# Attention with two gated layers on one core: a part of the probability transposes moved from the DMA queue to TensorE and ScalarE, with a new order

## The chip, the cores and the metric

The kernel runs on one core of a Trainium2 chip. The metric is the device time of one execution in microseconds. Engines: TensorE (PE in the profile), VectorE (DVE), ScalarE (ACT), GpSimd (POOL), and SyncE (SP), which here issues all DMA transfers.

## What is computed

```python
q_pool = q.reshape(B, H, S // 2, 2, D).mean(axis=3)          # B, H, S, D = 4, 8, 1152, 64
scores = D ** -0.5 * np.matmul(q_pool, k.transpose(0, 1, 3, 2))
scores = scores - np.max(scores, axis=-1, keepdims=True)
attn = np.exp(scores)
attn = attn / (np.sum(attn, axis=-1, keepdims=True) + 1e-09)
x = np.matmul(attn, v)                        # then (B, S/2, H, D) as 2304 tokens of 512
h = x @ w_in                                  # 512 -> 2048
x = (h * np.cos(h)) @ w_out                   # 2048 -> 512
return ((x @ w_a) * (x @ w_b)) @ w_out2       # 512 -> 1536 -> 512
```

## The kernel before

The run has two parts. In the **attention part** two heads form a pair p (16 pairs), and a pair has nine tiles of 128 pooled queries by 1152 keys; tile t (0 to 143) is number k = t % 9 of its pair, and the fifth (k = 4) has rows of both heads. Numbers are kept in two pieces, a high one and the rest (`kh`/`kl`, `vh`/`vl`), and products are summed over the pieces.

A tile goes through these steps, whose names are also those of the tasks:

- `s` (L316, TensorE): scores into one of two PSUM buffers of three banks, six products of 384 columns (twelve for k = 4).
- `max` (L324, VectorE), `exp` (L331, ScalarE, with the row sum; for half of the tiles it stays in the PSUM buffer, `in_psum`, t % 4 < 2, for the others it goes to SBUF as `pf`), `r1`/`r2` (VectorE, the reciprocal of the sum).
- `ph` (L346, ScalarE): the high half of the probabilities in f16, and `pl` (L350, VectorE): the low half. Both lie in one buffer `phl`, [128, 2, 1152]; there are four such buffers, so `ph` of a tile waits for the transpose of the tile four before.
- `tr` (L357, issued by SP): one DMA transpose of the whole `phl`, 18 blocks of 128x128, into `pt`, where the keys lie on the partitions. It also waits for the `av` of the pair before, which reads the same columns of `pt`.
- `av` (L373, TensorE): probabilities times values, twice per pair, 54 products each, from `pt` and `vh`/`vl`; read out by `avhi` (L383, ScalarE) and `avlo` (L392, VectorE) into the tokens `xt`.

Scores of tile t need the PSUM buffer of tile t - 2 back, from `pl` where the exponential stays in PSUM and from `exp` otherwise. Beside this run the loads of q, k, v (`qst`, `kst`, `vst`) with their splitting on GpSimd, VectorE and ScalarE (`kdup`, L222, is ScalarE's copy of k), the loads and conversion of `w_in` (`w`), and, from the fifth pair on, the first layer `h` (L448 to L450, TensorE, 12 products a group, 92 of its 128 groups here), read out by `ho` (L490) and stored by `hput` (L497). The groups of `av`, `h` and a small one for v share two PSUM slots (`mm_tile`): a third group waits until the first has been read out.

The **dense part** does the rest of the layers on TensorE; its code is not touched.

What sets the order: each step is a task with an engine, a cost and a due time, t plus a number of the table `DUE`. `Dag.run` plays the tasks through with these costs; whenever an engine is free it takes, of the tasks that are ready, the one that is due first, and the instructions are written in that order. On the chip each engine, and SP's queue, then goes through its list strictly in order; what is ready but stands behind a waiting instruction waits too. Groups in the two slots are tasks with `mm`.

Of the kernel before, what the change touches and what calls it, by code (L numbers as in the profile page):

```python
# [10 lines left out]
F16 = mybir.dt.float16  # L11
I32 = mybir.dt.int32
I64 = mybir.dt.int64
AF = mybir.ActivationFunctionType
ALU = mybir.AluOpType
# [10 lines left out]


DUE = dict(
    prep0=-6.24, prep1=-6.1, ldq=-38.55, ldk=-36.98, kd=-30.41, ldv=-79.38, qs=-131.27, vabs=17.17, vhi=75.51,
    vlo=70.05, max=-17.99, r=-31.13, exp=-1.94, ph=-23.98, pl=-7.26, tr=-30.08, av=-8.92, avh=22.89, avp=-196.82,  # L30
    xhi=-16.15, xlo=119.2, h=22.48, hrel=-90.16, whi=-65.72, wlo=-25.78, ho=-72.2, hput=60.89, w=51.54, slack=74.26,
    wstep=91.4
)


# [79 lines left out]
def kernel(  # L115
# [12 lines left out]
    nc = tc.nc  # L128
# [8 lines left out]
    TILES = 9  # L137
# [43 lines left out]
    def mm_tile(name):  # L181
        p = mm_slots[mm_at[0] % len(mm_slots)]
        mm_at[0] += 1
        return p.tile([128, 512], F32, tag="mm", name=name)
# [15 lines left out]

    ident = k_p.tile([128, 128], F32, name="ident")
    ones = k_p.tile([128, 128], F32R, name="ones")

    def v_const():
        nc.gpsimd.memset(ident, 1.0)
        nc.gpsimd.tensor_scalar(ones, ident, 1.0, 1.0, op0=ALU.mult, op1=ALU.mult)
        nc.gpsimd.affine_select(
            out=ident, in_=ident, pattern=[[-1, 128]], compare_op=ALU.is_equal,
            fill=0.0, base=0, channel_multiplier=1,
        )  # L210

    def load_k(p):
        b, pr = divmod(p, NP)
# [135 lines left out]
    def emit_pl(t):  # L349
# [2 lines left out]
            op0=ALU.mult, op1=ALU.subtract,  # L352
        )

    def emit_tr(t):
        k = t % TILES
        nc.sync.dma_start_transpose(  # L357
            out=pt[:, :, 128 * k:128 * k + 128],
            in_=phl_t.pop(t).rearrange("p a b c -> p (a b c)"),
        )  # L360

    av_ps = {}

# [143 lines left out]
    for c in range(C1):  # L507
        stages = convert(
            w_in[c], lambda: wf_p.tile([128, 512], F32, tag="wf", name="wf"),
            lambda t, c=c: w1.update({("i", c): t}), False,  # L510
        )
        at = DUE["w"] + DUE["wstep"] * c
        add(("w", c, 0), "SP", 1750, at, stages[0], deps=[("w", c - 1, 4)], wait=DMA_WAIT)
        for i, (eng, cost) in enumerate((("ACT", 650), ("DVE", 410), ("DVE", 680), ("DVE", 680))):
            deps = [("w", c, i)] + ([("w", c - 2, 3)] if i == 0 else [])
            add(("w", c, i + 1), eng, cost, at + 1 + i / 4, stages[i + 1], deps=deps, port=i > 0)
# [4 lines left out]
    for p in range(NPAIR):  # L521
        t0 = TILES * p
        b, pr = divmod(p, NP)
        for key, fn, cost, at, prev, free in (
            (("q", p), load_q, 2700, DUE["ldq"], ("v", p - 1), [("qlo", p - 1, 1)]),
            (("k", p), load_k, 2400, DUE["ldk"], ("q", p), [("klo", p - 1, 1), ("kdup", p - 1, 1)]),
            (("v", p), load_v, 2400, DUE["ldv"], ("k", p), [("vlo", p - 1)]),
        ):
            add(key, "SP", cost, t0 + at, fn, p, deps=free, after=[prev], wait=DMA_WAIT)
        add(("qs", p), "POOL", 1550, t0 + DUE["qs"], q_sum, p, deps=[("q", p)], slack=DUE["slack"])  # L530
# [16 lines left out]
        for k in range(TILES):  # L547
            t = t0 + k
            deps = [("pl" if in_psum(t - 2) else "exp", t - 2)]
            for j in ((0, 1) if k == 4 else (k // 5,)):  # L550
                deps += [("klo", p, j), ("kdup", p, j), ("qlo", p, j)]
            add(("s", t), "PE", (2100 if k == 4 else 1060) * (1.25 if p >= NP else 1.6), t, emit_s, t, deps=deps, after=[("s", t - 1)])
            add(("max", t), "DVE", 1340, t + DUE["max"], emit_max, t, deps=[("s", t)])
            stored = [u for u in range(t) if not in_psum(u)]
            free = [] if in_psum(t) or len(stored) < NPB else [("pl", stored[-NPB])]
            add(("exp", t), "ACT", 1420, t + DUE["exp"], emit_exp, t, deps=[("max", t)] + free)
            add(("r1", t), "DVE", 140, t + DUE["r"], emit_r1, t, deps=[("exp", t)])
            add(("r2", t), "DVE", 150, t + DUE["r"], emit_r2, t, deps=[("r1", t)])
            add(("ph", t), "ACT", 1240, t + DUE["ph"], emit_ph, t, deps=[("r2", t), ("tr", t - NPHL)], after=[("ph", t - 1)])
            add(("pl", t), "DVE", 1390, t + DUE["pl"], emit_pl, t, deps=[("ph", t)], port=not in_psum(t))  # L560
            deps = [("pl", t)]
            deps.append(("av", p - 1, 0 if k in (0, 1, 5) else 1))
            add(("tr", t), "SP", 3050, t + DUE["tr"], emit_tr, t, deps=deps, wait=DMA_WAIT)
        for hf in range(2):
            at = t0 + TILES + DUE["av"] + DUE["avh"] * hf
            deps = [("tr", t0 + k) for k in ((0, 1, 2, 4, 5, 6), (2, 3, 4, 6, 7, 8))[hf]]
            deps += [("vhi", p), ("vlo", p)]
            if b > 1:
                deps.append(("h", C1 * (b - 1) - 1, 1))
# [17 lines left out]
    for m in range(2 * H_CUT):  # L587
# [9 lines left out]
        deps = [("h", n, hf)] + ([("hput", n - NST)] if hf == 0 else [("ho", n, 0)])  # L597
        add(("ho", n, hf), "ACT", 400, at + DUE["ho"], h_out, n, hf, deps=deps, slack=DUE["slack"] / 4)
        if hf == 1:
            add(("hput", n), "SP", 1100, at + DUE["hput"], h_put, n, deps=[("ho", n, 1)], wait=DMA_WAIT)  # L600
    for n in range(H_CUT, H_CUT + 2):
        w_need(n)
    dag.run()
# [338 lines left out]
```

## Time and profile before

| | us |
|---|---|
| median of 3 runs | 1412.39 (1410.11 to 1415.44) |
| the profiled execution | 1420.35 |
| its span, first to last instruction | 1418.6 |

The profile is of one execution. Busy times are of engines that work side by side, so they don't add up to the span. A wait is put down to what ended it last; the chain of waits follows back from the last instruction what released each step. The DMA share is a mean over the 16 DMA engines of the time that their packets took; packets overlap, so it can pass 1. For SP's queue a transpose's time is how long it held the queue, and the landing is counted from its issue. The granted clock is a share of 2.4 GHz, at which TensorE runs at most; 0.5 is 1.2 GHz, the only other level seen here.

### The profile page before, as it was taken

To read this page: it belongs to the slowest core of one execution; us is meant where nothing else is said; L and a number is where in the kernel's file an instruction comes from. 1 tells how busy PE (TensorE), PEld (TensorE's weight loads), DVE (VectorE), ACT (ScalarE), POOL (GpSimd) and SP (SyncE) were. 2 spreads that over 40 slices of the span, in tenths; PEclk is the share of its full clock that TensorE was granted. 3 is DMA by queue.
4 is the path that set the end of the run, shared out by engine and by line. 5 is a ranking of instruction groups with operands and counts; after the bars stand their busy time and mean duration, and the time that the engine had idled before them with its cause. 6 is when DMAs were issued, how large, how long until landed. Compare 5 with 4: busy or idle time off the path is not lost.

```text
span 1418.6 us, 20183 instructions
## 1 busy us (share of the span) xinstructions
PE 1217.2 (86%) x7768; PEld 1139.6 (80%) x7768; DVE 905.2 (64%) x1304; ACT 755.9 (53%) x1134; POOL 415.1 (29%) x319
## 2 busy tenths in 40 slices
PE   3456668967689778976999999999999999999998
PEld 2445558856589768966999999999999999999997
DVE  6788888787878868887589999987411212111111
ACT  4567767776778657776486767764311111111111
POOL 5242334634437445640203434333100000000000
PEclk9668789988889989998999999999999999999999
DMA  5899999999989989998875466544010101010000
GB/s 169 162 190 206 199 197 203 229 222 192 217 174 232 220 172 213 212 229 157 247 233 164 155 196 201 192 152 135 30 67 0 67 1 67 0 67 0 23 1 23
DMA packets 380930, 206.33 MB, mean 145 GB/s; under 512 B 340641, under 2 KB 352929, under 8 KB 380321
## 3 DMA queue, kind: packets, MB, share of 16 engines
q1 hardware_dynamic: 380832, 205.03, 60.3%
q8 instruction: 61, 1.00, 0.3%
q14 instruction: 37, 0.29, 0.1%
HBM read 90.18 MB, written 29.88 MB: 85 GB/s over the span
## 4 chain that ended last, share of the span: by engine, by line
PE 61%; DVE 13%; issue 4%; ACT 3%; DMA 1%; POOL 1%; SPq 0%; DVEq 0%; ACTq 0%; POOLq 0%
PE s L316 6%; PE av L373 4%; DVE phl L350 4%; PE pa L448 4%; PE pa L450 4%; PE pa L449 4%; PE pb L450 4%; PE pb L449 4%; PE pb L448 4%; PE o L450 4%; PE o L449 4%; PE o L448 3%; PE h L448 3%; PE h L450 3%; PE h L449 3%
## 5 line engine op out<-in xcount | busy, mean ns | idle before, releaser
L316 PE MATMUL s<-kh,tq 128*128 128x384 f32 x480 | 190.7, 397 | 144.5 <-DVE phl L350 92.1
L316 PEld LDWEIGHTS s<-kh,tq 128*128 128x128 f32 x480 | 105.1, 219 | 167.4 <-issue 107.2
L718 DVE TENSOR_TENSOR pv<-pb,av 128x384 f32<-128x384 f32 x72 | 40.2, 558 | 300.5 <-PE pb L450 298.1
L324 DVE TENSOR_REDUCE nm<-s 128x1 f32<-128x1152 f32 x144 | 193.0, 1352 | 45.1 <-PE s L316 44.8
L316 PE MATMUL s<-kl,tq 128*128 128x384 f32 x480 | 181.1, 377 | 0.0
L448 PE MATMUL h<-xt,whl 128*128 128x288 f32 x512 | 156.6, 306 | 11.0 <-DVE vma L280 5.1
L450 PE MATMUL h<-xt,whl 128*128 128x288 f32 x512 | 154.7, 302 | 2.4 <-POOL whl L467 2.3
L449 PE MATMUL h<-xt,whl 128*128 128x288 f32 x512 | 154.2, 301 | 0.0
L714 ACT ACTIVATE av<-pa 128x384 f32<-128x384 f32 x72 | 35.5, 493 | 204.9 <-PE pa L450 204.8
L448 PE MATMUL x<-gh,w 128*128 128x384 f32 x384 | 130.6, 340 | 5.6 <-DVE x2t L686 5.6
L449 PE MATMUL x<-gl,w 128*128 128x384 f32 x384 | 130.5, 340 | 3.2 <-DVE gl L655 3.2
L331 ACT ACTIVATE pf<-s,nm 128x1152 f32<-128x1152 f32 x72 | 88.0, 1223 | 81.6 <-DVE nm L324 81.2
L450 PE MATMUL x<-gh,w 128*128 128x384 f32 x384 | 130.1, 339 | 0.0
L350 DVE SCALAR_TENSOR_TENSOR phl<-pf,rc,phl 128x1152 f16<-128x1152 f32 x72 | 119.8, 1671 | 9.4 <-ACT phl L346 9.3
L373 PE MATMUL av<-pt,vh 128*64 128x288 f16 x1152 | 121.2, 301 | 4.0 <-DMA pt<-phl 3.8
L722 ACT ACTIVATE ph<-pv 128x384 fp32r<-128x384 f32 x72 | 37.9, 527 | 145.9 <-DVE pv L718 145.9
L350 DVE SCALAR_TENSOR_TENSOR phl<-s,rc,phl 128x1152 f16<-128x1152 f32 x72 | 100.9, 1412 | 22.7 <-ACT phl L346 22.5
L448 PEld LDWEIGHTS h<-xt,whl 128*128 128x128 f32 x512 | 99.7, 195 | 14.0 <-issue 9.9
L316 PEld LDWEIGHTS s<-kl,tq 128*128 128x128 f32 x480 | 106.1, 221 | 0.0
L450 PEld LDWEIGHTS h<-xt,whl 128*128 128x128 f32 x512 | 99.4, 194 | 3.5 <-POOL whl L467 3.4
L331 ACT ACTIVATE s<-s,nm 128x1152 f32<-128x1152 f32 x72 | 85.8, 1192 | 28.3 <-DVE nm L324 27.0
L449 PEld LDWEIGHTS h<-xt,whl 128*128 128x128 f32 x512 | 99.7, 195 | 0.0
(88 smaller groups left out, 3208.1 us busy)
## 6 DMA issues: line engine op xcount, KB each, us to landing
h_d<-hs SPq DMA_DIRECT2D x64, 288.0 KB, 2.7
gf<-h_d SPq DMA_DIRECT2D x48, 384.0 KB, 3.4
raw<-in_w_out_dram SPq DMA_DIRECT2D x28, 512.0 KB, 4.1
qst<-in_qT_dram SPq DMA_DIRECT2D x16, 640.0 KB, 4.9
kst<-in_kT_dram SPq DMA_DIRECT2D x16, 576.0 KB, 5.0
vst<-in_vP_dram SPq DMA_DIRECT2D x16, 576.0 KB, 4.7
raw<-in_w_in_dram SPq DMA_DIRECT2D x16, 512.0 KB, 4.1
raw<-in_w_a_dram SPq DMA_DIRECT2D x12, 512.0 KB, 4.3
```

The costliest lines, as they stand in the source:

```text
L316: nc.tensor.matmul(ps[:, c, :N3], lhs, kx[:, c * N3:(c + 1) * N3], start=(i == 0), stop=(i == len(terms) - 1),)
L324: nc.vector.tensor_reduce(nm, s_t[t][:, :, :N3], op=ALU.max, axis=AX.XY, negate=True)
L331: nc.scalar.activation(pf, ps, AF.Exp, bias=m_t.pop(t), scale=1.0, accum_out=rs)
L350: nc.vector.scalar_tensor_tensor(phl_t[t][:, 1], e_t.pop(t)[0], rc_t.pop(t), phl_t[t][:, 0], op0=ALU.mult, op1=ALU.subtract,)
L373: nc.tensor.matmul(ps[64 * j:64 * j + 64, :NH], vx[:, kt, 64 * j:64 * j + 64], pt[:, o + kt, c0:c0 + NH], start=(kt == 0 and i == 0), stop ...
L448: nc.tensor.matmul(ps, lh, rh, start=first, stop=False)
L449: nc.tensor.matmul(ps, lh, rl, start=False, stop=False)
L450: nc.tensor.matmul(ps, ll, rh, start=False, stop=last)
L714: nc.scalar.activation(ab_t["a"], p_ps.pop("a")[:, :T2], AF.Copy, scale=W_INV)
L718: nc.vector.tensor_tensor(ab_t[at, c], p_ps.pop("b")[:, :T2], ab_t.pop("a"), op=ALU.mult)
L722: nc.scalar.activation(ph_t[at, c][:, 0], ab_t[at, c], AF.Copy)
```

## The change

In every third tile (t % 3 == 2, 48 of 144) the DMA transposes only the low half, nine blocks. The high half is transposed by TensorE: three groups `tp` of three products each, the 128x128 block as the stationary operand times a f16 identity (`ident16`, made once on GpSimd), into one of the two shared PSUM slots; ScalarE copies each group, 128x384, into `pt` (`te`). A group needs only `ph`, not `pl`. `ph` of a tile that reuses the buffer waits for the products as well as for the transpose, and `av` waits for the copies. The code also allows the low half (with VectorE), which is not used.

The planner's costs of SP's transfers are raised (a whole transpose 3050 to 3350, a half 1700; loads of q, k and v by 300, of w by 350, stores by 250), and nearly all numbers of `DUE` are different, so that every engine's order changes. The lines that matter:

```diff
 DUE = dict(
-    prep0=-6.24, prep1=-6.1, ldq=-38.55, ldk=-36.98, kd=-30.41, ldv=-79.38, qs=-131.27, vabs=17.17, vhi=75.51,
+    prep0=-9.26, prep1=2.27, ldq=-30.55, ldk=-36.98, kd=-30.63, ldv=-67.47, qs=-117.71, vabs=22.98, vhi=69.7,
...
+    wstep=44.21, tp=0.33, te=-16.64,
 )
...
+    ident16 = k_p.tile([128, 128], F16, name="ident16")
...
+        nc.gpsimd.tensor_scalar(ident16, ident, 1.0, 1.0, op0=ALU.mult, op1=ALU.mult)
...
+    def by_pe(t):
+        return (0,) if t % 3 == 2 else ()
+
     def emit_tr(t):
         k = t % TILES
-        nc.sync.dma_start_transpose(
-            out=pt[:, :, 128 * k:128 * k + 128],
-            in_=phl_t.pop(t).rearrange("p a b c -> p (a b c)"),
-        )
+        cols = slice(128 * k, 128 * k + 128)
+        if by_pe(t):
+            nc.sync.dma_start_transpose(
+                out=pt[:, KT:, cols], in_=phl_t[t][:, 1].rearrange("p b c -> p (b c)")
+            )
+        else:
+            nc.sync.dma_start_transpose(
+                out=pt[:, :, cols], in_=phl_t[t].rearrange("p a b c -> p (a b c)")
+            )
+
+    def emit_tp(t, e, i):
+        tp_ps[t, e, i] = mm_tile("tp")
+        for n in range(3):
+            cols = slice(128 * n, 128 * n + 128)
+            nc.tensor.matmul(
+                tp_ps[t, e, i][:, cols], phl_t[t][:, e, i, cols], ident16, start=True, stop=True
+            )
+
+    def emit_te(t, e, i):
+        k = t % TILES
+        src = tp_ps.pop((t, e, i))[:, :384].rearrange("p (n c) -> p n c", n=3)
+        dst = pt[:, e * KT + 3 * i:e * KT + 3 * i + 3, 128 * k:128 * k + 128]
+        if e == 0:
+            nc.scalar.activation(dst, src, AF.Copy)
+        else:
+            nc.vector.tensor_scalar(dst, src, 1.0, None, op0=ALU.mult)
...
-        add(("w", c, 0), "SP", 1750, at, stages[0], deps=[("w", c - 1, 4)], wait=DMA_WAIT)
+        add(("w", c, 0), "SP", 2100, at, stages[0], deps=[("w", c - 1, 4)], wait=DMA_WAIT)
...
-            (("q", p), load_q, 2700, DUE["ldq"], ("v", p - 1), [("qlo", p - 1, 1)]),
+            (("q", p), load_q, 3000, DUE["ldq"], ("v", p - 1), [("qlo", p - 1, 1)]),
...
-            add(("tr", t), "SP", 3050, t + DUE["tr"], emit_tr, t, deps=deps, wait=DMA_WAIT)
+            if len(by_pe(t)) < 2:
+                add(("tr", t), "SP", 1700 if by_pe(t) else 3350, t + DUE["tr"], emit_tr, t, deps=deps, wait=DMA_WAIT)
+            for e in by_pe(t):
+                for i in range(3):
+                    add(("tp", t, e, i), "PE", 300, t + DUE["tp"] + i / 10, emit_tp, t, e, i,
+                        deps=[("pl" if e else "ph", t), ("tp", t, e, i - 1), deps[1]], mm=("te", t, e, i))
+                    add(("te", t, e, i), "DVE" if e else "ACT", 450, t + DUE["te"] + i / 10, emit_te, t, e, i,
+                        deps=[("tp", t, e, i), deps[1]])
...
+            deps += [("te",) + d[1:] + (e, i) for d in deps for e in range(2) for i in range(3)]
...
-            add(("hput", n), "SP", 1100, at + DUE["hput"], h_put, n, deps=[("ho", n, 1)], wait=DMA_WAIT)
+            add(("hput", n), "SP", 1350, at + DUE["hput"], h_put, n, deps=[("ho", n, 1)], wait=DMA_WAIT)
```

The two other loads, k and v, change as the load of q does, and `ph` gets the products of the tile four before among its dependencies.

Two places show how the order moves. First SP's queue from the transpose of tile 94 to the load of k for pair 12 (`kst`); `x2` counts equal rows, `128x18x128` is a whole transpose, `128x9x128` a half. Before (the rows ahead of these are stores of `h`):

```order
L357 DMA_TRANSPOSE pt<-phl 128x18x128 x2
L255 DMA vst<-in_vP_dram 128x1152
L357 DMA_TRANSPOSE pt<-phl 128x18x128 x2
L231 DMA qst<-in_qT_dram 128x1280
L357 DMA_TRANSPOSE pt<-phl 128x18x128 x3
L215 DMA kst<-in_kT_dram 128x1152
L497 DMA h_d_60<-hs 128x576
```

Now (from the transposes of tiles 93 and 94 on):

```order
L370 DMA_TRANSPOSE pt<-phl 128x18x128 x2
L526 DMA h_d_60<-hs 128x576 x2
L366 DMA_TRANSPOSE pt<-phl 128x9x128
L370 DMA_TRANSPOSE pt<-phl 128x18x128
L257 DMA vst<-in_vP_dram 128x1152
L370 DMA_TRANSPOSE pt<-phl 128x18x128
L526 DMA h_d_60<-hs 128x576
L366 DMA_TRANSPOSE pt<-phl 128x9x128
L233 DMA qst<-in_qT_dram 128x1280
L370 DMA_TRANSPOSE pt<-phl 128x18x128 x2
L217 DMA kst<-in_kT_dram 128x1152
```

The load of k stays behind the transpose of tile 100, but two of the seven transposes from tile 94 on are halves; the load of v moves behind tile 96, and three stores of `h` stand among them.

Second ScalarE, from the exponential of tile 100 on; `phl` is a high half, `hs` a read-out of `h`, `xt` one of `av`. Before:

```order
L331 ACTIVATE s,rs<-s,nm 128x3x384
L346 ACTIVATE phl<-pf,rc 128x1152
L331 ACTIVATE s,rs<-s,nm 128x3x384
L383 ACTIVATE xt_2_119<-av,viv 128x288
L346 ACTIVATE phl<-s,rc 128x1152 x2
L331 ACTIVATE pf,rs<-s,nm 128x1152 x2
L346 ACTIVATE phl<-pf,rc 128x1152
```

Now (`pt<-tp` is the copy of a transposed group):

```order
L333 ACTIVATE s,rs<-s,nm 128x3x384
L412 ACTIVATE xt_2_119<-av,viv 128x288
L387 ACTIVATE pt<-tp 128x3x128
L348 ACTIVATE phl<-pf,rc 128x1152
L348 ACTIVATE phl<-s,rc 128x1152
L387 ACTIVATE pt<-tp 128x3x128 x2
L333 ACTIVATE s,rs<-s,nm 128x3x384
L519 ACTIVATE hs<-h 128x288
L348 ACTIVATE phl<-s,rc 128x1152
L412 ACTIVATE xt_2_119<-av,viv 128x288
L387 ACTIVATE pt<-tp 128x3x128
```

The copies of tile 98 stand between the exponentials of tiles 100 and 101, one ahead of two high halves and two directly ahead of the exponential.

## Rows read from the trace of the kernel before

**Rows 1.** The page, parts 1 and 2: busy time by engine; granted clock and DMA by slice.
```profile
PE 1217.2 (86%) x7768; PEld 1139.6 (80%) x7768; DVE 905.2 (64%) x1304; ACT 755.9 (53%) x1134; POOL 415.1 (29%) x319
...
PEclk9668789988889989998999999999999999999999
DMA  5899999999989989998875466544010101010000
```

**Rows 2.** Stretches of the run, columns named in the header row.
```profile
core 0: us, PE busy (x) PEld busy (x) DVE busy (x) ACT busy (x) POOL busy (x), PEclk, DMA share, GB/s
27.00:212.00 185.00, 109.35 (x732) 94.17 (x733) 154.80 (x230) 123.20 (x159) 58.64 (x39) 0.76 0.94 191
212.00:400.00 188.00, 143.73 (x1055) 130.52 (x1054) 155.89 (x230) 134.94 (x190) 83.39 (x63) 0.87 1.00 211
400.00:683.00 283.00, 238.45 (x1944) 221.75 (x1944) 220.16 (x321) 201.01 (x290) 143.35 (x111) 0.94 0.97 202
683.00:1419.00 736.00, 721.04 (x4031) 689.17 (x4029) 359.30 (x505) 286.06 (x484) 110.57 (x89) 0.99 0.29 95
...
0.00:242.00 242.00, 142.04 (x993) 124.75 (x994) 193.75 (x283) 155.47 (x204) 94.20 (x71) 0.82 0.89 189
242.00:683.00 441.00, 354.16 (x2749) 325.70 (x2749) 352.16 (x517) 314.40 (x447) 210.31 (x160) 0.90 0.98 205
```

**Rows 3.** Chain of waits: the whole run by engine; 242 to 683 us by line.
```profile
PE 61%; DVE 13%; issue 4%; ACT 3%; DMA 1%; POOL 1%; SPq 0%; DVEq 0%; ACTq 0%; POOLq 0%
...
by line: PE s L316 19.0%; PE av L373 12.7%; DVE phl L350 11.6%; DVE nm L324 9.8%; issue 9.5%; PE h L448 6.7%; PE h L450 6.4%; PE h L449 6.1%; DVE tq L245 2.8%; ACT pf L331 2.3%; ACT phl L346 1.9%; POOL whl L467 1.4%; DVE vl L303 1.3%; POOL 
```

**Rows 4.** Waits from 27 to 683 us: who waited for whom, us, times, longest.
```profile
PEld s L316 <- issue: 107.2, 30, 9.3
...
PE s L316 <- DVE phl L350: 92.1, 18, 9.0
ACT pf L331 <- DVE nm L324: 81.2, 56, 5.8
...
ACT s L331 <- DVE nm L324: 16.8, 19, 1.8
```

**Rows 5.** The transposes by DMA: ns min, median, max; issue to landing.
```profile
L357 SPq DMA_TRANSPOSE pt<-phl x144: 2406/2852/4735, 27.0 to 677.9; - x144
...
DMA to landing us min/median/max: 4.5/4.8/8.0
```

**Rows 6.** SP's queue in order of time, 460 to 500 us.
```profile
start us, us, engine line op out<-in xcount [idle before <-releaser]
...
461.13 5.81 SPq L357 DMA_TRANSPOSE pt<-phl  x2
467.03 0.71 SPq L255 DMA_DIRECT2D vst<-in_vP_dram  x1
467.85 7.90 SPq L357 DMA_TRANSPOSE pt<-phl  x2
475.85 0.52 SPq L231 DMA_DIRECT2D qst<-in_qT_dram  x1
476.47 11.01 SPq L357 DMA_TRANSPOSE pt<-phl  x3
487.53 0.57 SPq L215 DMA_DIRECT2D kst<-in_kT_dram  x1
```

**Rows 7.** ScalarE in order of time, behind that load.
```profile
489.36 1.20 ACT L331 ACTIVATE s<-s,nm 128x1152 f32<-128x1152 f32 x1
...
492.89 1.16 ACT L222 ACTIVATE kh<-kst 64x1152 fp32r<-64x1152 f32 x1 [2.22 <-DMA kst<-in_kT_dram]
...
494.38 1.25 ACT L346 ACTIVATE phl<-pf,rc 128x1152 f16<-128x1152 f32 x1
```

**Rows 8.** Longest pieces of the chain of waits: start us, us, what.
```profile
276.22 3.43 PE av L373 x54
...
411.57 1.06 PE s L316 x6
...
487.53 5.34 DMA kst<-in_kT_dram
...
640.66 4.54 DMA pt<-phl
```

**Rows 9.** Groups of instructions, 27 to 683 us: count, busy us, mean ns, idle before.
```profile
L273 PE MATMUL vb<-vdg,ones 128*128 128x128 f32 x15 | 4.4, 292 | 7.6 <-ACT vdg L268 7.5
```

**Rows 10.** A copy of 128x384 out of PSUM by ScalarE, whole run.
```profile
L714 ACT ACTIVATE av<-pa 128x384 f32<-128x384 f32 x72 | 35.5, 493 | 204.9 <-PE pa L450 204.8
```

More of the change, by code (lines that the diff above doesn't have):

```diff
@@ L28 @@
 DUE = dict(
-    prep0=-6.24, prep1=-6.1, ldq=-38.55, ldk=-36.98, kd=-30.41, ldv=-79.38, qs=-131.27, vabs=17.17, vhi=75.51,
-    vlo=70.05, max=-17.99, r=-31.13, exp=-1.94, ph=-23.98, pl=-7.26, tr=-30.08, av=-8.92, avh=22.89, avp=-196.82,
-    xhi=-16.15, xlo=119.2, h=22.48, hrel=-90.16, whi=-65.72, wlo=-25.78, ho=-72.2, hput=60.89, w=51.54, slack=74.26,
-    wstep=91.4
+    prep0=-9.26, prep1=2.27, ldq=-30.55, ldk=-36.98, kd=-30.63, ldv=-67.47, qs=-117.71, vabs=22.98, vhi=69.7,
+    vlo=61.68, max=-13.91, r=-34.75, exp=5.22, ph=-25.64, pl=2.02, tr=-29.93, av=-4.35, avh=22.18, avp=-192.9,
+    xhi=-15.47, xlo=104.36, h=39.46, hrel=-84.65, whi=-53.72, wlo=-23.45, ho=-74.26, hput=63.79, w=29.14, slack=0,
+    wstep=44.21, tp=0.33, te=-16.64,
 )
@@ L353, in emit_pl @@
         )
+    tp_ps = {}
+    def by_pe(t):
+        return (0,) if t % 3 == 2 else ()
     def emit_tr(t):
         k = t % TILES
-        nc.sync.dma_start_transpose(
-            out=pt[:, :, 128 * k:128 * k + 128],
-            in_=phl_t.pop(t).rearrange("p a b c -> p (a b c)"),
-        )
+        cols = slice(128 * k, 128 * k + 128)
[22 more added lines that the diff above has]
+            nc.vector.tensor_scalar(dst, src, 1.0, None, op0=ALU.mult)
     av_ps = {}
@@ L524 @@
         for key, fn, cost, at, prev, free in (
-            (("q", p), load_q, 2700, DUE["ldq"], ("v", p - 1), [("qlo", p - 1, 1)]),
-            (("k", p), load_k, 2400, DUE["ldk"], ("q", p), [("klo", p - 1, 1), ("kdup", p - 1, 1)]),
-            (("v", p), load_v, 2400, DUE["ldv"], ("k", p), [("vlo", p - 1)]),
+            (("q", p), load_q, 3000, DUE["ldq"], ("v", p - 1), [("qlo", p - 1, 1)]),
+            (("k", p), load_k, 2700, DUE["ldk"], ("q", p), [("klo", p - 1, 1), ("kdup", p - 1, 1)]),
+            (("v", p), load_v, 2700, DUE["ldv"], ("k", p), [("vlo", p - 1)]),
         ):
@@ L558 @@
             add(("r2", t), "DVE", 150, t + DUE["r"], emit_r2, t, deps=[("r1", t)])
-            add(("ph", t), "ACT", 1240, t + DUE["ph"], emit_ph, t, deps=[("r2", t), ("tr", t - NPHL)], after=[("ph", t - 1)])
+            add(("ph", t), "ACT", 1240, t + DUE["ph"], emit_ph, t, deps=[("r2", t), ("tr", t - NPHL)] + [("tp", t - NPHL, e, 2) for e in range(2)], after=[("ph", t - 1)])
             add(("pl", t), "DVE", 1390, t + DUE["pl"], emit_pl, t, deps=[("ph", t)], port=not in_psum(t))
```

## Prediction

> **What bounds the kernel now.** I read the stretches first. From 683 us on, TensorE is busy 721 of 736 us [rows 2]: that dense part is bound by it, and the change doesn't touch it. What can move lies in the attention part, 27 to 683 us, 656 us for 144 tiles, 4.56 us each. No engine is full there: TensorE 75%, VectorE 81%, ScalarE 70% (sums of the first three stretches over 656), but the DMA engines show a share of 0.94 to 1.00 [rows 1, 2]. Two readings compete. By the DMA share the transposes hold the pace. By the chain of waits they do not: between 242 and 683 us its time lies on TensorE (`s` 19.0, `av` 12.7, `h` 19.2%, together 51%) and VectorE (the low half, L350, and the maximum, L324: 21%), and over the whole run DMA is 1% of it, 14 us [rows 3]. The waits say the same: `s` waits 92 us for L350, the exponentials 98 us for the maximum [rows 4]. So the part is a loop with two score buffers in PSUM: scores, maximum, exponential, high half, low half, then the scores of the tile after next; four engines take turns, and the in-order queues decide who is late.
>
> The DMA queue enters through lateness. SP issues in order, and a transpose holds it 2.85 us at the median [rows 5]. Look at 461 us: seven transposes with two loads between them keep SP until 487.53, and only then goes the next `kst` load [rows 6]. Its landing is a piece of the chain, 5.34 us [rows 8]; ScalarE stands 2.22 us before the copy L222, and the next high half, at 494.38, stands behind it [rows 7]. So removed transposes are worth more than the 14 us that carry DMA's name, and less than their full time.
>
> **The change part by part.** *Removed.* In 48 of the 144 tiles the DMA moves half as much. Half of 2.85 us is 1.43; 48 times that is 68 us off SP's queue. Upper end: all 68, if the DMA share is right. Lower end: DMA's 14 us shrink by the sixth of the transposed bytes that goes, 2 us. The share (near 1) is nearest to the upper end, the chain to the lower; I take the middle, **minus 34**. The order bears it out at the place above: from the first of those seven transposes to the `kst` load two are now halves, so the load goes out some 2.9 us earlier, more than the 2.22 us ScalarE waited for it.
>
> *Added on TensorE.* 48 tiles times 3 groups times 3 products, 432 products of 128x128, f16, each with its own weight load. Lower bound: six score products of 384 columns take 1.06 us [rows 8], so 128 columns cost 59 ns, 0.18 us a group, 26 us in all. Upper bound: the lone 128x128 product takes 292 ns [rows 9], 126 us in all. The nearest row is `av`: f16, a weight load each, 54 in 3.43 us, 64 ns [rows 8]; but its weights are 64 columns wide, and 128 could take twice that, 127. I take 96 ns, 0.29 us a group, 42 us. On the path: two thirds of it falls after 242 us, where TensorE has 51% of the chain: 14 us. Before that it is busy 142 of 242 us, against 354 of 441 after [rows 2]; no chain is shown there, and I take half the share for 14 us of products, 4 us. **Plus 18**, with 11 to 54 by the two bounds at the same share, 0.43. Below nothing is possible too: TensorE had 0.76 of its clock from 27 to 212 us and 0.94 where it was busier [rows 2]; were it 1.0 there, 109 busy us would shrink by at most a quarter, 26 us, and at 0.25 on the path give back 6.
>
> *Added on ScalarE.* 144 copies of 128x384 out of PSUM. The row with that shape takes 493 ns [rows 10]: 71 us, on an engine that is busy 459 of the 656 us [rows 2]. In the new order 79 of the 144 stand, alone or in a run, directly ahead of an exponential. What hides them is the maximum: the exponentials wait for it 75 times, 98 us, 1.3 us each [rows 4], and a run of three copies is 1.5 us. ScalarE's share of the chain is 4.2% [rows 3], of 71 us that is **plus 3**; the other end is 79 copies uncovered, 39 us.
>
> *The new wait.* A group takes one of two PSUM slots which the products of `h`, `av` and the groups share; the third group of a tile needs the first one's slot back. In 18 of 48 tiles the three stand back to back on TensorE. The third could start 0.58 us after the first; the first is free after 0.29 + 0.49 and a hand-over each way, some 0.9: 0.3 us, 18 times, 5 us, of which half on the path, **plus 3**. In the other 30 tiles scores, `av` or `h` stand between, 1.06 us or more [rows 8]; without that cover all 48 would lose 14 us. Queued behind a waiting group on TensorE are scores, and VectorE waits for those.
>
> *Moved.* The table of due times and SP's costs are new, so every queue is reordered: loads, stores of `h`, the tails. Both orders have the same 84 of 92 `h` groups ahead of the last score tile, but the new one spreads them more evenly (20 against 26 done by tile 71, 76 against 83 by tile 131). No row prices an order. The longest single wait that the profile can't explain is 9.3 us [rows 4]; one such place more or fewer is **0, plus or minus 9**. VectorE's work is unchanged.
>
> Sum: -34 + 18 + 3 + 3 + 0 = -10 us. The profiled execution took 1420.35 us (span 1418.6); by this it becomes 1410. The median of the shown runs, 1412.39, lies 8.0 us lower, and I put the same difference on it: 1402.
>
> **A rule that speaks against it.** The Trainium skill, TensorE: Matmul & The Clock Gate, Part 4: PE-mode transpose, gives about 275 ns for a transpose of 128x128 on TensorE inside a kernel. By that figure, as an estimate, the products are 119 us instead of 42. The trace has a product of that size at 292 ns when it stands alone, and f16 products at 64 ns when they follow each other, and here three or more follow each other; no run so far shows which holds.
>
> **The rivals.** *The loop keeps the pace.* VectorE is busy 84% from 27 to 212 us and 83% from 212 to 400 [rows 2], its work stays, and the two score buffers stay. Then the emptier DMA queue only waits longer for low halves, and the added work on TensorE and ScalarE goes into their idle time: about nothing either way, 1412. For it: the chain. Against: the queue's lateness above.
>
> *ScalarE's order turns it round (slower).* Mechanism: a copy stands ahead of an exponential, but its products are queued on TensorE behind scores or `av` (3.43 us [rows 8]), so the copy is late and holds the exponential, the high half and the loop. Price: 0.49 us for each such copy. The sum reaches zero when 10 + 3 = 13 us of copies lie on the loop, 27 of the 79; with 40 of them it is 1419, with all 79 (39 us) 1438. Taken: 1425.
>
> *Products at the lone price.* If each of the 432 costs 292 ns, TensorE gets 126 us, at 0.43 on the path 54: -34 + 54 + 6 = +26, 1438. By the Trainium skill's figure above it would be 1435.
>
> *The DMA holds the pace.* All 68 us count: -68 + 24 = -44, 1368. For it: the share of 1.00 from 212 to 400 us. Against: DMA's 1% of the chain.
>
> *A half costs a whole.* If a transpose of half the columns holds the queue as long, nothing is removed and 24 us are added: 1436. The fastest of 144 equal ones took 2.41 us, the slowest 4.74 [rows 5], so other traffic moves the time, which speaks for a rate and against a fixed cost.
>
> **How the numbers follow.** Chances: forecast (about -10, between -24 and +2) 0.40; loop keeps the pace 0.22; ScalarE's order 0.15; products at the lone price 0.08; DMA holds the pace 0.11; half costs a whole 0.04. 0.5%, about what a measurement of this kernel can tell from no change, is 7 us: faster means under 1405, slower over 1419. Faster: three quarters of the forecast's 0.40, the 0.11, and 0.04 of the loop's: 0.45. Slower: 0.08 + 0.04, 0.13 of ScalarE's 0.15, 0.05 of the loop's: 0.30. Same: 0.25. The range leaves out the larger part of the DMA rival below, 0.07, and the dear products and whole-cost halves above, 0.12: 1372 to 1430.
>
> **What would show it.** In the profile of after: transposes of half size near 1.4 us on SP, and a DMA share clearly under 0.9 from 27 to 400 us, confirm the first term; the same share with shorter time confirms the DMA rival. Product groups of 0.2 to 0.4 us confirm the second. Exponentials that wait for copies, or scores that wait for a copy, show the rival on ScalarE. The end of the last tile's transpose, now 683 us, should come near 673; the dense part should keep its 736 us. I am wrong if that part moves, if VectorE is above 88% busy and the end of attention doesn't move, or if TensorE waits for ScalarE more than some 20 us in all.

## The result

The change made the kernel slower. The median was 1432.12 us (1429.23 to 1434.55) against 1413.91 of the kernel before, run beside it: a ratio of 1.0126, 95% interval 1.0094 to 1.0157. Forecast were 1402 us, range 1372 to 1430. The profiled execution has a span of 1431.8 us, against 1418.6.

Parts 1 and 2 of the page of the changed kernel, to be read beside [rows 1]: busy time by engine, granted clock and DMA share by slice.

```profile
PE 1259.0 (88%) x8200; PEld 1169.9 (82%) x8200; DVE 898.0 (63%) x1304; ACT 810.0 (57%) x1278; POOL 426.0 (30%) x320
...
PEclk9677779998999999898999999999999999999999
DMA  5879879997878888886676456544110101010000
```

The stretches of the changed kernel, as in [rows 2]; the last two rows cut the run at 696 us, where the last transpose has landed.

```profile
core 0: us, PE busy (x) PEld busy (x) DVE busy (x) ACT busy (x) POOL busy (x), PEclk, DMA share, GB/s
27.00:212.00 185.00, 127.08 (x844) 106.98 (x845) 151.62 (x231) 139.10 (x198) 56.97 (x37) 0.74 0.83 170
212.00:400.00 188.00, 150.95 (x1202) 136.14 (x1201) 156.53 (x233) 151.02 (x233) 93.25 (x66) 0.94 0.88 188
400.00:683.00 283.00, 243.82 (x1985) 223.78 (x1984) 213.07 (x312) 215.73 (x338) 139.17 (x103) 0.92 0.82 173
27.00:696.00 669.00, 533.74 (x4146) 477.89 (x4147) 525.06 (x780) 513.13 (x780) 294.40 (x209) 0.87 0.84 176
696.00:1400.00 704.00, 693.94 (x3906) 663.68 (x3905) 353.30 (x496) 280.87 (x475) 112.11 (x90) 1.00 0.30 98
```

The DMA did become emptier: 0.94, 1.00 and 0.97 of [rows 2] are now 0.83, 0.88 and 0.82. The attention part became longer all the same, 669 us where it was 656. TensorE is busy 533.7 us of it, so idle 135.3; before it was busy 491.5 and idle 164.5 (sums of [rows 2]). The idle time fell by 29 us, the busy time rose by 42.

The two kinds of transpose of the changed kernel, each in the view of its line (ns: min, median, max; first and last issue), as in [rows 5].

```profile
L370 SPq DMA_TRANSPOSE pt<-phl x96: 2417/2788/4717, 27.0 to 688.0; - x96
```

```profile
L366 SPq DMA_TRANSPOSE pt<-phl x48: 1242/1310/2097, 36.1 to 690.8; - x48
...
DMA to landing us min/median/max: 3.2/3.5/5.8
```

A half holds SP 1.31 us, less than half of a whole. The last transpose is issued at 690.8 us, 12.9 later than the 677.9 of [rows 5] (it should have come earlier: the last landing was forecast near 673 us and came near 696); the span is 13.2 us longer. (The medians differ by 18; the profiled execution of before was one of its slower ones.) So the loss lies in the attention part, and the dense part kept its length.

Who waited for whom in the changed kernel, 27 to 700 us (us, times, longest), as in [rows 4].

```profile
PE s L318 <- DVE phl L352: 46.4, 19, 8.8
ACT pf L333 <- DVE nm L326: 46.0, 40, 4.2
...
PE tp L378 <- ACT pt L387: 13.7, 16, 4.0
PE tp L378 <- ACT phl L348: 12.9, 6, 4.2
PE h L477 <- ACT pt L387: 12.4, 10, 2.2
...
ACT pt L387 <- PE tp L378: 12.0, 17, 1.9
```

The new work of the changed kernel in the same stretch, grouped by line (count, busy us, mean ns of one, idle ahead of it), with the small product for v.

```profile
L387 ACT ACTIVATE pt<-tp 128x384 f16<-128x384 f32 x144 | 65.7, 490 | 12.6 <-PE tp L378 12.0
L378 PE MATMUL tp<-ident,phl 128*128 128x128 f16 x432 | 48.1, 239 | 34.8 <-ACT pt L387 13.7 <-ACT phl L348 12.9 <-DVE xt L421 4.4
...
L275 PE MATMUL vb<-vdg,ones 128*128 128x128 f32 x15 | 4.4, 292 | 3.7 <-ACT pt L387 3.7
```

The old waits of [rows 4] halved (92.1 to 46.4 and 81.2 to 46.0). In their place TensorE waits for ScalarE's copies: products 13.7, `h` 12.4 and the product for v 3.7 us, together 29.8. ScalarE in its turn waits 12.0 us for products. These rows show that the new steps hold each other up, but not what the time would be without that; the runs below do.

### The profile page after: what moved, and what is told of

It reads as the page before. It is cut to its first block, busy times and chain, and to the rows that moved or that the text cites. A ratio compares the mean times of both kernels' runs of the same rounds, so it can differ in the third digit from the quotient of the medians.

```text
span 1431.8 us, 21127 instructions
## 1 busy us (share of the span) xinstructions
PE 1259.0 (88%) x8200; PEld 1169.9 (82%) x8200; DVE 898.0 (63%) x1304; ACT 810.0 (57%) x1278; POOL 426.0 (30%) x320
## 4 chain that ended last, share of the span: by engine, by line
PE 46%; DVE 5%; ACT 2%; issue 1%; DMA 1%; SPq 0%; DVEq 0%; ACTq 0%
PE pa L477 4%; PE pa L479 4%; PE pa L478 4%; PE pb L477 4%; PE pb L479 3%; PE pb L478 3%; PE o L479 3%; PE o L478 3%; PE o L477 3%; PE x L477 3%; PE x L478 3%; PE x L479 3%; PE h L477 1%; PE h L479 1%; PE h L478 1%
## 5 line engine op out<-in xcount | busy, mean ns | idle before, releaser
L318 PE MATMUL s<-kh,tq 128*128 128x384 f32 x480 | 195.4, 407 | 86.7 <-DVE phl L352 46.4
L318 PEld LDWEIGHTS s<-kh,tq 128*128 128x128 f32 x480 | 108.0, 225 | 100.6 <-ACT pf L333 30.8
L318 PE MATMUL s<-kl,tq 128*128 128x384 f32 x480 | 184.7, 385 | 0.0
L477 PE MATMUL h<-xt,whl 128*128 128x288 f32 x512 | 158.4, 309 | 16.3 <-ACT pt L387 12.4
L352 DVE SCALAR_TENSOR_TENSOR phl<-pf,rc,phl 128x1152 f16<-128x1152 f32 x72 | 111.4, 1551 | 8.3 <-ACT phl L348 8.1
L333 ACT ACTIVATE pf<-s,nm 128x1152 f32<-128x1152 f32 x72 | 88.1, 1224 | 46.4 <-DVE nm L326 46.0
```

Of the source, the lines that this page charges most:

```text
L318: nc.tensor.matmul(ps[:, c, :N3], lhs, kx[:, c * N3:(c + 1) * N3], start=(i == 0), stop=(i == len(terms) - 1),)
L333: nc.scalar.activation(pf, ps, AF.Exp, bias=m_t.pop(t), scale=1.0, accum_out=rs)
L352: nc.vector.scalar_tensor_tensor(phl_t[t][:, 1], e_t.pop(t)[0], rc_t.pop(t), phl_t[t][:, 0], op0=ALU.mult, op1=ALU.subtract,)
L477: nc.tensor.matmul(ps, lh, rh, start=first, stop=False)
```

## The experiments

Runs made at different times had slightly different medians of the kernel before, so kernels are compared by their ratio to it. "Scale" is that ratio times 1413 us.

| run | order | transposes | in their place | median us | ratio (95%) | scale us |
|---|---|---|---|---|---|---|
| after | new | halves | products, copies | 1432.1 | 1.0126 (1.0094 to 1.0157) | 1430.8 |
| a3 | new | whole | nothing | 1444.4 | 1.0209 (1.0177 to 1.0241) | 1442.5 |
| a1 | new | halves | nothing | 1425.4 | 1.0072 (1.0046 to 1.0099) | 1423.2 |
| a2 | new | halves | products | 1418.4 | 1.0024 (1.0010 to 1.0038) | 1416.4 |
| c1 | new | halves | products of a constant | 1418.8 | 1.0037 (1.0021 to 1.0053) | 1418.2 |
| d1 | new | halves | products, copies of a constant | 1420.0 | 1.0031 (1.0010 to 1.0052) | 1417.4 |
| b1 | old | halves | nothing | 1416.5 | 1.0022 (1.0001 to 1.0043) | 1416.1 |
| b2 | old table, planned again | halves | products, copies | 1444.9 | 1.0208 (1.0162 to 1.0254) | 1442.4 |
| b3 | new table, planned again | whole | nothing | 1531.5 | 1.0832 (1.0788 to 1.0875) | 1530.6 |
| o1 | searched for the old method | whole | nothing | 1409.1 | 0.9956 (0.9940 to 0.9971) | 1406.8 |
| o1h | that of o1 | halves | nothing | 1403.4 | 0.9924 (0.9898 to 0.9950) | 1402.3 |
| o3 | searched for the old method | whole | nothing | 1423.9 | 1.0057 (1.0038 to 1.0077) | 1421.1 |
| n1 | searched for the change | halves | products, copies | 1414.4 | 0.9987 (0.9971 to 1.0004) | 1411.2 |
| n2 | searched for the change | halves | products, copies | 1414.6 | 0.9988 (0.9973 to 1.0003) | 1411.3 |
| n1h | that of n1 | halves | nothing | 1400.9 | 0.9907 (0.9874 to 0.9940) | 1399.9 |
| n1p | that of n1 | halves | products | 1398.9 | 0.9876 (0.9857 to 0.9895) | 1395.5 |
| n1d | that of n1 | halves | products, copies of a constant | 1404.7 | 0.9919 (0.9900 to 0.9938) | 1401.6 |

**The order alone, the halves alone.** a3 writes the instructions in the changed kernel's order but does the old work:

```diff
-        if by_pe(t):
-            nc.sync.dma_start_transpose(
-                out=pt[:, KT:, cols], in_=phl_t[t][:, 1].rearrange("p b c -> p (b c)")
...
+        nc.sync.dma_start_transpose(
+            out=pt[:, :, cols], in_=phl_t[t].rearrange("p a b c -> p (a b c)")
+        )
...
     def emit_tp(t, e, i):
+        pass
...
     def emit_te(t, e, i):
+        pass
```

a1 keeps the halves and has the two `pass`. b1 is the kernel before, in its order, with halves at `t % 3 == 2` and nothing in their place.

Kernels without copies leave out the high half of every third tile. Where nothing is written there (a1, a2, c1, b1, n1h, n1p, o1h) it is set to zero once, on GpSimd, in b1 here:

```profile
16.52 3.06 POOL L229 MEMSET pt<- 128x1152 f16 x3
```

The first high half then comes some 2 us later: at 26.2 us in b1 and 24.3 before, at 26.4 in a1 and 24.5 in a3, at 26.2 in a2 and 24.1 in d1 (26.4 in n1p and 23.7 in n1d; in o1h only 0.2 later than in o1). A step from one kind of kernel to the other can be off by that much.

> The changed kernel with its order kept, but all 144 transposes are whole again by DMA and there are no products and copies: the work of the kernel before in the new order. Theory A: the order is not the cause, 1405 to 1415 us, as before, and some 15 us above the run with halves alone. Theory B: 1425 us or more.

> The changed kernel with its order kept, but the 432 products and the 144 copies are left out; the 48 half transposes stay (the high half of every third tile is zeros, so that part of the result is missing). Theory A (the products and copies hold up the loop through ScalarE's order and the two PSUM slots): 1385 to 1400 us, 30 us or more under the changed kernel's 1432. Theory B (the new order itself is worse, the products and copies lie in idle time): 1420 to 1430 us.

> The kernel before with its order kept; every third transpose moves only the low half and nothing takes the place of the high half (zeros, that part of the result is missing): the price of the DMA time by itself. My prediction's first term says minus 34 us, 1380; the chain of waits (lower end) minus 2, 1410; the DMA share (upper end) minus 68, 1345. Theory A says 1385 to 1400; theory B says nothing of this run.

The same work as before, in the new order, takes 30 us more (1442.5 against 1413). From there the halves bring 19 us back, and products with copies cost 8 again: 29.5 - 19.3 + 7.6 is the loss of 17.8. a1 and a3 came out as Theory B had it, the new order itself is worse. In the old order the halves bring nothing: 3 us on the slow side, of which the zeros can be 2.

The same two steps can be taken the other way round, halves first: +3 (before to b1), and then the order +7 (b1 to a1, 1416.1 to 1423.2). Order and halves together cost 10 us either way, but the order's share is 30 with whole transposes and 7 with the halves that it was made for. These runs give the sum, not one price for each.

The stretches of b1, two of its groups of waits, and then the waits for `kst` before:

```profile
27.00:212.00 185.00, 108.81 (x731) 93.00 (x732) 156.54 (x232) 124.64 (x160) 61.26 (x39) 0.77 0.81 171
212.00:400.00 188.00, 141.68 (x1046) 128.90 (x1045) 155.10 (x224) 132.13 (x185) 86.17 (x63) 0.86 0.86 185
400.00:683.00 283.00, 243.07 (x1959) 226.43 (x1958) 222.92 (x327) 203.25 (x295) 149.48 (x111) 0.92 0.86 183
```

```profile
PE s L319 <- DVE phl L353: 94.4, 19, 10.7
...
POOL kh L219 <- DMA kst<-in_kT_dram: 11.1, 4, 4.6
```

```profile
POOL kh L219 <- DMA kst<-in_kT_dram: 18.6, 6, 6.9
...
ACT kh L222 <- DMA kst<-in_kT_dram: 3.2, 3, 2.2
```

The DMA share fell to 0.81, 0.86 and 0.86, and the lateness on which the first term was argued [rows 6, 7] shrank: GpSimd waits 11.1 us for the loads of k instead of 18.6, and ScalarE no longer does. But the scores wait 94.4 us for the low halves, as before [rows 4], and the time stays. In that order the queue was late and full, and yet not what held the loop.

The stretch from 27 us to the last landing in a3, then in a1:

```profile
27.00:706.00 679.00, 509.69 (x3718) 462.74 (x3718) 533.45 (x781) 459.18 (x637) 294.15 (x211) 0.85 0.94 194
```

```profile
27.00:686.00 659.00, 499.12 (x3719) 453.34 (x3719) 530.20 (x781) 458.88 (x638) 296.00 (x210) 0.86 0.84 179
```

a3 has TensorE busy 509.7 us with 3718 products, where [rows 2] sum to 491.5 us with 3731: 18 us more for the same work, at a mean granted clock of 0.85, and only 5 us more idle time. The worse order showed as slower products, far more than as idle time.

**The planner's table.** b3 plans the old method with the new table and costs (`by_pe` returns `()`); b2 plans the change with the old ones:

```diff
 DUE = dict(
-    prep0=-9.26, prep1=2.27, ldq=-30.55, ldk=-36.98, kd=-30.63, ldv=-67.47, qs=-117.71, vabs=22.98, vhi=69.7,
+    prep0=-6.24, prep1=-6.1, ldq=-38.55, ldk=-36.98, kd=-30.41, ldv=-79.38, qs=-131.27, vabs=17.17, vhi=75.51,
...
-                add(("tr", t), "SP", 1700 if by_pe(t) else 3350, t + DUE["tr"], emit_tr, t, deps=deps, wait=DMA_WAIT)
+                add(("tr", t), "SP", 1550 if by_pe(t) else 3050, t + DUE["tr"], emit_tr, t, deps=deps, wait=DMA_WAIT)
```

> All transposes whole by DMA, planned anew with the changed table of due times and the changed costs of SP's transfers: replanning alone, without products and copies in the plan. Theory A: within 1 per cent of before, 1400 to 1420 us. Theory B (table and costs are worse): 1425 us or more.

> The whole change, planned with the due times and costs of the kernel before (the two new due times kept, a half transpose at half the old cost of a whole). Theory A, that the old table holds the better order whatever is planned with it: halves alone took 1416 us in the old order, products and copies 7 us more in the new one, so 1420 to 1427 us. Theory B, that a table is fitted to the very set of steps it was found for (the old method planned with the new table and costs took 1532 us): slower than the change under its own table, 1435 to 1460 us, with TensorE's waits for phl above the 46 us of the changed kernel.

Both are slow, b3 by 118 us. With another set of steps the same numbers give another order, and in both cases here it was a worse one. Of the waits for `phl` that b2's expectation named, scores did not wait longer for low halves (40.6 against 46.4 us in the changed kernel), but products waited longer for high halves (37.0 against 12.9). In b2, 27 to 703 us:

```profile
PE s L318 <- DVE phl L352: 40.6, 19, 8.2
PE tp L378 <- ACT phl L348: 37.0, 9, 6.7
```

Then tables were searched anew, for either method. Nothing but `DUE` differs from the changed kernel (n1, n2) or from the kernel before (o1, o3). The table of o1:

```diff
+    prep0=66.5, prep1=125.6, ldq=349.98, ldk=-179.89, kd=-329.25, ldv=-801.24, qs=-277.61, vabs=-10.01,
+    vhi=-230.44, vlo=138.37, max=-304.56, r=-391.22, exp=-24.25, ph=-139.58, pl=-246.36, tr=-173.62, av=14.18,
+    avh=3.06, avp=-540.72, xhi=-152.67, xlo=1432.53, h=86.79, hrel=-1061.39, whi=-460.79, wlo=-137.8, ho=-352.04,
+    hput=500.37, w=203.2, slack=78.76, wstep=137.82,
```

and the first and the last line of n1's:

```diff
+    prep0=22.91, prep1=150.15, ldq=-14.08, ldk=-38.66, kd=-200.83, ldv=-75.84, qs=166.82, vabs=14.36, vhi=224.22,
...
+    w=278.37, slack=6.85, wstep=364.72, tp=2.12, te=-252.44,
```

> The changed kernel with nothing but the table of due times exchanged, for one searched anew for this set of steps; half transposes, products, copies and planning costs are the same. Theory A, the order is what the change lost by (the new order carrying the old work took 31 us more than the old order): those come back, 1432 - 31 = 1401 us, 1392 to 1415 us. Theory B, the products and copies themselves make the loss, since TensorE must wait for phl, for a PSUM tile and for ScalarE wherever they stand (some 90 us of such waits at the products' groups in the changed kernel): 1425 to 1435 us, whatever the table.

> The kernel before with nothing but its table of due times exchanged, for one searched anew in the same way; its work is the same, all transposes whole and by DMA. It tells whether an order still to be had is worth as much to the old method as to the new. Theory A, the order sets the time of either method: 1395 to 1408 us, with TensorE's wait of s for phl below the 92 us of before. Theory B, the order of before is already as good as this method allows, and only fewer transposed bytes give more: 1409 to 1418 us, or more.

> The changed kernel with a second searched table in place of n1's. n1 and o1 are one table for each method; a second of each shows how much of the 5 us between them is the method's. Theory A, the method costs about 5 us with fitted tables: 1410 to 1420 us here. Theory B, single tables scatter by as much as the methods differ: 1400 to 1410 us here, or above 1422.

> The kernel before with a second searched table in place of o1's. Theory A, the method costs about 5 us with fitted tables: 1404 to 1414 us here, below n2. Theory B, single tables scatter by as much as the methods differ: above 1416, or above n2.

The table alone takes the changed kernel from 1430.8 to 1411.2 us on the scale: 20 us, and the loss is gone; its median, 1414.4, lies at the slow end of the 1392 to 1415 that were expected if the order was the whole loss. o1 beats both kernels, the one before by 0.44% (0.29 to 0.60), with the work of the kernel before. But o3, a second table for the old method, is slower than before, and the two of the change agree with each other and lie between: so these four don't tell which method is better at its best. That stays open.

The stretch from 27 us to the last landing in n1, with its old and new waits (27 to 683 us):

```profile
27.00:673.00 646.00, 517.31 (x4131) 459.68 (x4130) 530.26 (x780) 510.37 (x779) 288.85 (x208) 0.90 0.87 182
```

```profile
PE s L318 <- DVE phl L352: 41.0, 22, 8.5
...
PE tp L378 <- ACT pt L387: 12.2, 18, 1.3
...
ACT pt L387 <- PE tp L378: 10.2, 12, 1.9
...
PE h L477 <- ACT pt L387: 7.0, 9, 1.3
```

Beside the changed kernel's 669 us: busy 517 instead of 534, idle 129 instead of 135, granted clock 0.90 instead of 0.87.

**Products and copies apart.** a2 is a1 with the products put back. c1 differs from a2 in one line, d1 in the step `te` (which writes a constant, so it needs no zeros):

```diff
# c1
-                tp_ps[t, e, i][:, cols], phl_t[t][:, e, i, cols], ident16, start=True, stop=True
+                tp_ps[t, e, i][:, cols], ident16, ident16, start=True, stop=True
...
# d1
-        tp_ps.pop((t, e, i))
+        k = t % TILES
+        src = ident16.unsqueeze(1).broadcast_to([128, 3, 128])
+        dst = pt[:, e * KT + 3 * i:e * KT + 3 * i + 3, 128 * k:128 * k + 128]
+        nc.scalar.activation(dst, src, AF.Copy)
```

> The changed kernel's order with the products in place and ScalarE's copies left out (the high half of every third tile stays zero). Without products and copies this order took 1425 us, with both 1432 us; this run splits the 7 us. Theory A, the products cost them by standing in TensorE's row and waiting there for a free PSUM tile: 1429 to 1433 us, the wait of the products for phl stays near 30 us, the wait for the copies goes. Theory B, the copies cost them, by holding exp and ph back on ScalarE (70.6 us of work) and by holding PSUM tiles for the products: 1422 to 1427 us.

> As a2 (the changed order, products without copies), but each product is of the identity with itself, so that no product waits for phl; the high half of every third tile stays zero. In a2 the products made the order 7 us faster than without them (1418 against 1425 us), with the granted clock from 27 to 683 us up (0.72/0.89/0.93 to 0.77/0.94/0.96). Theory A, the products' work keeps TensorE's clock up and that is where the 7 us come from: 1408 to 1418 us with the clock at a2's level, and what it is below a2 is the price of the wait for phl. Theory B, the 7 us come from the products' waits (they bring TensorE to its next step later and so in better step with the others): back to 1423 to 1428 us.

> As a2, with ScalarE's copies put back, but reading a constant in SBUF in place of the products' PSUM tiles: the same 144 instructions of 128x384 on ScalarE, which hold no PSUM tile and wait for no product; the high half of every third tile holds the constant. a2 took 1418 us, the whole change 1432 us. Theory A, ScalarE's time is the cost (144 x 0.49 = 71 us that exp and ph wait for): 1428 to 1434 us. Theory B, the tie between TensorE and ScalarE is (a product waits for the PSUM tile until the copy two steps back is done, a copy waits in ScalarE's row for its product): 1417 to 1423 us.

The products alone make the order 7 us **faster** (1423.2 to 1416.4); neither of a2's two theories had allowed for less than 1422. The stretch of a2, beside that of a1 above, and the products of a2 and of c1, 27 to 700 us:

```profile
27.00:679.00 652.00, 520.69 (x4148) 465.97 (x4149) 527.72 (x781) 458.61 (x638) 295.75 (x210) 0.90 0.86 181
```

```profile
L381 PE MATMUL tp<-ident,phl 128*128 128x128 f16 x432 | 46.9, 238 | 18.5 <-ACT phl L351 16.1 <-DVE xt L418 0.6 <-ACT pf L336 0.2
```

```profile
L381 PE MATMUL tp<-ident 128*128 128x128 f16 x432 | 46.4, 233 | 2.7 <-DVE xt L418 1.0 <-DVE vma L285 0.2
```

46.9 of the 520.7 busy us are products; the rest, 474 us, is what took 499 us in a1, at a granted clock of 0.86 instead of 0.90. TensorE's idle time fell too, from 160 to 131 us. So of the 47 us of products 29 went into idle time, 18 would have come on top, and the 25 us less of the other work turn that into a gain of 7. With c1 no product waits for `phl`, and the time is the same within the intervals: those waits neither cost nor gained anything. That leaves the clock as the likely source of the gain; no run holds the clock and adds the products, so it is argued and not shown. This is the "below nothing" that the prediction gave 6 us as the farthest.

d1 puts ScalarE's work back, and costs 1 us more than a2 (up to 3 without a2's zeros), too little to tell from none; the whole change costs 13 more than d1. So most of the copies' price is the **tie**: a PSUM tile is held until ScalarE has copied it, and a copy stands in ScalarE's row until its product is done. ScalarE's own time for the copies, 66 to 69 us, found idle time. d1's copies and its waits for them, by line (27 to 700 us) and by who waited (27 to 683 us):

```profile
L386 ACT ACTIVATE pt<-ident 128x384 f16<-128x384 f16 x144 | 68.7, 515 | 0.1
```

```profile
ACT phl L348 <- ACT pt L386: 1.6, 4, 0.6
...
PEld L378 <- ACT pt L386: 0.5, 2, 0.3
```

And the stretch of d1:

```profile
27.00:682.00 655.00, 519.97 (x4145) 464.33 (x4146) 527.21 (x780) 514.45 (x780) 293.71 (x209) 0.90 0.86 179
```

Against it the changed kernel is idle equally long (135 us in both) and busy 14 us longer with the same products, at 0.87 instead of 0.90. Here the tie, too, came out as busy time at a lower clock. Why the clock is lower with the tie at the same idle time, these runs don't show; nor do they part the two directions of the tie, since d1 takes away both.

**The same in the searched orders.**

> The order of n1 (the change with the table searched anew, 1414 us) without products and copies; halves stay, the high half of every third tile is left zero. Theory A, products and copies cost in any order: 1400 to 1410 us. Theory B, in an order fitted to them the clock that the products hold up pays for them (in the changed kernel's order the products alone gained 7 us and the copies lost 14): 1411 to 1418 us.

> As a2, in the order of n1: products without copies; the high half of every third tile stays zero. In the first order the products alone gained 7 us, by the granted clock. Theory A, they gain here too: 1390 to 1398 us. Theory B, they gain only where TensorE's clock was low; n1 without them had 0.75/0.89/0.96, against 0.72/0.89/0.93 in the first order, so little is left to gain: 1398 to 1405 us.

> As d1, in the order of n1: products in place, ScalarE's copies reading a constant in SBUF, so that no PSUM tile is held by a copy; the high half of every third tile holds the constant. n1 took 1414 us, the same order without products and copies 1401 us, so they cost 13.5 us there. Theory A, the tie through PSUM is the cost in this order too, as in the first (12 of the 14 us of the copies there): 1399 to 1405 us. Theory B, n1's order is fitted to the tie, and ScalarE's 71 us are the cost: 1410 to 1416 us.

> The order of o1 (the kernel before with a table searched anew, 1409 us) with a half in place of each third whole transpose and nothing in its place; the high half of every third tile is left zero. It repeats on a second order what b1 showed on the first. Theory A, the queue's relief is worth nothing by itself in an order planned for whole transposes: 1406 to 1412 us. Theory B, b1 was one order's accident (the first order of the change gained 19 us by its halves): 1390 to 1402 us.

n1h has the edit of a1 in n1's order, n1p that of a2, n1d that of d1; o1h has that of b1 in o1's order. Steps on the scale: products -4 us (not sure, the intervals overlap), the copies' time +6 (up to 9 without n1p's zeros), the tie +10, together +11. n1h came out as its Theory A had it (1400 to 1410), n1p at the lower end of its Theory B (1398 to 1405), and n1p is the fastest of all. The stretch to the last landing in n1p, then in n1d:

```profile
27.00:661.00 634.00, 517.75 (x4147) 457.48 (x4149) 533.10 (x782) 458.20 (x638) 293.35 (x211) 0.91 0.91 186
```

```profile
27.00:665.00 638.00, 515.43 (x4142) 456.65 (x4141) 533.82 (x780) 511.97 (x780) 291.49 (x209) 0.90 0.90 184
```

n1d, at 1404.7, came out at the upper end of its Theory A: in a fitted order the tie is still the larger share, but ScalarE's time is no longer free. Here the tie came out differently: against n1d, n1 is idle 6 us longer (129 against 123) and busy 2, both at 0.90. So a tie cost 13 and 10 us in two orders, once as a lower clock and once mostly as idle time.

o1h fell between its two theories. It is 4.5 us faster than o1, though the intervals overlap, against 3 us slower in b1: half transposes are worth about 0, 5 and 19 us in three orders, nowhere the 34 of the forecast. Its stretch:

```profile
27.00:668.00 641.00, 488.72 (x3709) 443.54 (x3709) 524.96 (x779) 458.07 (x636) 288.59 (x210) 0.86 0.88 184
```

## Why the prediction was wrong

Wrong in sign. Its steps, beside what the runs gave in the changed kernel's order:

| term | forecast | measured | by |
|---|---|---|---|
| half transposes | -34 (-68 to -2) | -19; in the old order +3 | a3 to a1; b1 |
| order | 0, plus or minus 9 | +30; with the halves there +7 | before to a3; b1 to a1 |
| (both together) | -34 | +10 | before to a1 |
| products | +18 (11 to 54) | -7 | a1 to a2 |
| copies' time | +3 (0 to 39) | +1 | a2 to d1 |
| new wait | +3 (0 to 14) | +13 | d1 to after |
| sum | -10 | +18 | |

- **The step that failed** is the first term, minus 34 for the half transposes, with the order that came with them put at 0. Together they measured +10, 44 us off; products, copies and wait measured +8 where +24 was forecast, which hid 16 of the error. That was luck: their own terms were off too.
- **What bounds the kernel** was read rightly: the loop of four engines, not the DMA. But then the first term was put in the middle between the DMA share and the chain. In the old order the chain was right: b1 gives +3, up to 2 of it from the zeros, nearest to the term's lower end of 2 us gained. In the new order the same halves were worth 19, within the range but taken from an order that is 30 us worse with whole transposes. The place at 461 us, a load that came 2.2 us late, was real and was mended (in the changed kernel ScalarE waits for no `kst`), but one late step in a loop with slack elsewhere is not a price for the 68 us.
- **The order** cost 7 to 30 us, by what runs in it. "No row prices an order" was true, and the 9 us taken for it was the longest single wait, which has nothing to do with it. A new table of 30 numbers can move every wait of the loop at once: the runs that exchanged or re-planned it went from 1407 to 1531 us.
- **The products** were priced well as instructions: 48.1 us in all against 42, 111 ns each against 96. The Trainium skill, TensorE: Matmul & The Clock Gate, Part 4: PE-mode transpose, gives about 275 ns; here products follow each other and the measured 48.1 us decide against it. The same part of the Trainium skill says that transposes in TensorE's own mode don't bring up the clock. These are ordinary products with an identity, and the clock was higher with them, 0.90 against 0.86 (a2, a1). On the path the forecast of +18 agrees, by the count above, with what did not go into idle time in a2; what it had wrong is the rest of TensorE's work, which became 25 us shorter. The prediction had seen such a gain, at most 26 us from 27 to 212 us, but let only a quarter of it count and left it out of the sum.
- **The copies** as instructions cost 65.7 us against 71, and their time was hidden in this order, as forecast.
- **The new wait** was named, and sized too small. Counted were only the third groups behind two others, 18 times 0.3 us. The rows show 16 waits of products, mean 0.86 us, and 14 more of `h` and the product for v, which share the two tiles and had been left out, and 17 waits of ScalarE for its products. The 5 us so counted were then halved; the runs give 13.
- **The signs that were named**: the half at 1.31 us (1.4 said), the DMA share under 0.9, the product group at 0.33 us (48.1 / 144; 0.2 to 0.4 said) and the unchanged dense part all came true, and the time rose. "Confirms the first term" was the wrong reading of the share: it confirms that the work left the queue, not that the queue's work was on the path. The sign that spoke against, TensorE waiting for ScalarE more than 20 us, came true with 29.8 us for the copies alone. As it was worded it could not tell: before the change scores already waited longer than that for exponentials (27 to 683 us).

```profile
PE s L316 <- ACT pf L331: 32.3, 29, 2.8
```

- **The rivals**: in time the two at 1436 and 1438 were nearest to 1432, but their mechanisms did not occur: a half holds the queue 1.31 us, and a product group took 0.33 us. That ScalarE's order turns it round (1425 us) had half of the mechanism: late copies, with their price through the PSUM tiles and not ahead of exponentials. "The loop keeps the pace" describes b1.

## What to carry to other kernels

Where a planner or a table sets the order, run the old work in the new order, and the new transfers in the old order beside it. Two kernels then tell how far method and order can be priced apart at all; here the same halves were worth 19 us in one order and nothing in the other. A full queue is a bound only if work waits for it: in the old order the DMA share fell from 0.94 and more to 0.86 and less, and the time stayed. Moving work between engines adds a hand-over each way; here it cost 13 us (10 in a second order) where the copies' own time cost 1 (6), and part of the waits fell on `h` and the product for v, which only share the buffers.

## What was not expected of the hardware

In the changed kernel's order the granted clock of TensorE moved with the time. With 432 added products the attention part was shorter, and the other work went from 499 to 474 us as the granted clock rose from 0.86 to 0.90 (a1 to a2). About the same number of products took 491.5 us in one order and 509.7 in another, at 0.87 and 0.85 (before and a3). These means lie between the two levels, 1.2 and 2.4 GHz. The clock doesn't rank the kernels, though: o1h took 1402 us at 0.86, the changed kernel 1431 at 0.87.

A half transpose holds SP's queue 1.31 us and lands after 3.5, a whole one 2.79 and 4.8 (medians of the changed kernel): with half the bytes it held the queue a little under half as long, and took almost three quarters of the time to land.
